# Output weights split in the dense part, two more pairs of tiles turned by DMA, and a new order of the last part

## The chip, the core and the metric

The kernel runs on one core of one Trainium2 chip. The metric is the device time of one execution in microseconds, as the median of the runs. Beside it stands one profiled execution, whose trace gives all the rows below. In the rows PE is TensorE, PEld its weight loads, DVE is VectorE, ACT is ScalarE, POOL is GpSimd and SP is SyncE, which issues most of the transfers.

## The reference

```python
x = A_x                                            # 1 x 2048 x 640
g = sigmoid((x * gate_w).sum(-1, keepdims=True))
q, k, v = heads(x @ wqkv)                          # 32 heads of 20
pq, pk = q @ w_phi, k @ w_phi                      # per head
phi_q = concat(softmax(pq), softmax(-pq))          # 40 per head
phi_k = concat(softmax(pk), softmax(-pk))
kv, z = phi_k^T v, sum(phi_k)                      # per head
o = (phi_q @ kv) / (phi_q @ z + 1e-6)
a = o @ wo
b = silu(x @ w1) @ w2                              # 640 -> 1728 -> 640
return g * a + (1 - g) * b
```

## The kernel before

All matrices are float32. Where full accuracy is wanted an operand is split in two parts: ScalarE casts it to a high part, and GpSimd or VectorE subtracts to get the low part; TensorE then makes three products in place of one.

The program runs in this order: the keys, values and kv of all 16 tiles of 128 rows (order KV); the dense part b (HEAD, O1 to O10, each of them one pair of w1's column tiles beside the products with w2 of the pair before); then TAIL, which ends the dense part and makes the query features of the tiles 12 to 15; and FIN, which makes those of the tiles 0 to 11 and all the output. Rows are handled in eight pairs of tiles (256 rows). PB gives their order: pair 0 of FIN's count is the tiles 12 and 13, pair 1 the tiles 14 and 15, pairs 2 to 7 the tiles 0 to 11.

Each of these parts is an order written out by hand, a string of step names. A step issues its instructions when its name is reached, and a chain of dependencies keeps every engine in that order (in TAIL and FIN also SP's queue, in the dense part not SP). An engine that waits holds back all that stands behind it on that engine, and nothing on the others.

The query features of a tile t: q_proj (TensorE, 30 matmuls, steps qp12 to qp15 and q0p to q11p), q_max and q_sub (VectorE, from PSUM), q_exp (ScalarE), q_sum and q_norm_sum (VectorE), q_norm (GpSimd, the product with z), q_parts, q_inv and q_weights (small ones), q_mul (GpSimd, qm and q0M and so on). The features must then be turned, so that heads lie on partitions. There are two ways. A pair in TPOSE is turned by TensorE: t_mm makes 22 transposes into banks of PSUM, and t_out evicts them on ScalarE. For any other pair q_out (steps qg12, q0g and so on) copies the features on ScalarE as 16-bit halves and writes them to m_d in DRAM, from ScalarE's queue; three transfers q_in (steps such as j0, j12) bring them back turned, from SP's queue.

From the turned features n_mm (steps n00 to n04 for pair 0, four matmuls each) makes the heads' outputs, n_hi and n_lo (h, l) evict them to oT as high and low part, and r_mm, r_hi, r_lo (z0m, z0h, z0l) do the same for a rest of the heads, which r_store writes to r_d and r_place (z0d) brings from there into the gap rows of oT. Both pn and rest tiles are taken from the PSUM tag single, with four banks, as are the output's. When all of a block of oT is there (two pairs, 512 columns, for the blocks 0 to 2; one pair for 3 and 4), w_mm multiplies with wo (steps w00a to w44b), w_add adds b, and w_out stores.

The output weights wo are loaded in TAIL (wo_load, five chunks of 128 rows), split by ScalarE and GpSimd (wo_split), and kept in one large tile, which takes a buffer that the last inputs of the dense part hold until hm013.

Pools used by the change: raw (four tiles for unsplit inputs), w (nine large slots for weights and features), x (seven slots for split inputs).

## Time and profile before

| | us |
|---|---|
| median of 3 runs | 702.77 (702.6 to 703.48) |
| the profiled execution | 704.52 |
| its span, from the first to the last instruction | 702.6 |
| TensorE busy in the span | 694.7 |
| VectorE, GpSimd, ScalarE busy | 464.4, 395.5, 309.4 |
| granted clock of TensorE, mean | 0.998 of full |

The time of the profiled execution is 1.9 us over its span; the median of the runs is 0.2 us over that span. The profile is read in three ways here: the share of each engine, which tells who is busy; the same by stretches, which tells where TensorE has room; and the chain of work that ended last, which tells what released each piece of it. A time in the trace counts from the first instruction of the span.

### The profile page before, as it was taken

The page shows a single profiled execution, that of the slowest core. Times are in us where ns is not written, and L with a number is a line of the kernel's source. Part 1 is how long each engine was busy: PE and PEld are TensorE (multiplying, and loading weights), DVE is VectorE, ACT ScalarE, POOL GpSimd, SP SyncE. Part 2 cuts the span into 40 slices and gives each one's busy share as a digit, 9 for nine tenths or more (in the row PEclk, how much of TensorE's full clock was granted, in tenths as well). Part 3 has the DMA queues.
Part 4 walks back from the last instruction along what each step waited for, and adds up shares of the span by engine and source line. Part 5 has one row for each costly group of instructions (what it writes and reads, how often), then busy time and mean ns, then how long its engine had stood idle before and what let it go on. Part 6 is the DMA issues. An engine that isn't in the chain of part 4 may idle for free.

```text
span 702.6 us, 11974 instructions
## 1 busy us (share of the span) xinstructions
PE 694.7 (99%) x4536; PEld 589.1 (84%) x4536; DVE 464.4 (66%) x769; ACT 309.4 (44%) x552; POOL 395.5 (56%) x303
## 2 busy tenths in 40 slices
...
GB/s 307 144 170 293 310 292 298 280 275 237 184 284 146 199 240 231 73 190 240 298 243 245 139 153 126 78 207 261 35 52 140 111 157 202 211 257 209 218 142 132
DMA packets 88631, 140.70 MB, mean 200 GB/s; under 512 B 38466, under 2 KB 52054, under 8 KB 88574
## 3 DMA queue, kind: packets, MB, share of 16 engines
...
q14 instruction: 21, 0.17, 0.1%
...
## 4 chain that ended last, share of the span: by engine, by line
PE 95%; DMA 2%; DVE 1%; ACT 1%; SPq 0%; issue 0%; DVEq 0%; ACTq 0%
PE kvp L621 18%; PE o L1196 11%; PE o L1237 11%; PE pa L1834 10%; PE a L1107 10%; PE pq L597 9%; PE ph L687 3%; PE b L1107 3%; PE c L1107 3%; PE d L1107 3%; PE o_m L1259 3%; PE pn L1756 2%; PE hp L706 2%; PE kvt L608 2%; DMA oT<-r_d 1%; PE kvp L492 1%
## 5 line engine op out<-in xcount | busy, mean ns | idle before, releaser
L1227 DVE TENSOR_TENSOR acc<-acc,o 128x512 f32<-128x512 f32 x104 | 68.4, 683 | 35.3 <-PE o L1237 35.1
L621 PE MATMUL kvp<-wh,xa 128*128 128x480 f32 (+2 forms) x420 | 90.3, 358 | 0.0
L621 PEld LDWEIGHTS kvp<-wh,xa 128*128 128x128 f32 x420 | 72.8, 188 | 10.0
L1196 PE MATMUL o<-u,w 128*128 128x512 f32 x340 | 80.7, 390 | 0.0
L1834 PE MATMUL pa<-oT,wo 128*128 128x512 f32 (+1 forms) x375 | 73.8, 354 | 2.3 <-DMA oT<-r_d 2.3
L1196 PEld LDWEIGHTS o<-u,w 128*128 128x128 f32 x340 | 63.6, 188 | 13.6 <-DVE acc L1201 0.3
L1834 PEld LDWEIGHTS pa<-oT,wo 128*128 128x128 f32 x375 | 60.5, 191 | 14.0 <-ACT eq L1334 2.3
L1351 POOL TENSOR_TENSOR ez<-eq,zbc 128x1280 f32<-128x1280 f32 x16 | 47.6, 2974 | 22.3 <-ACT eq L1334 17.5
L1123 POOL TENSOR_TENSOR u<-v,u 128x512 fp32r<-128x512 f32 x16 | 20.7, 1296 | 64.0 <-ACT u L1122 64.0
L649 POOL TENSOR_TENSOR ek<-ek,st 128x1280 f32<-128x1280 f32 x16 | 38.3, 2397 | 30.8 <-DVE st L648 18.9
L1121 ACT ACTIVATE v<-v 128x512 f32<-128x512 f32 x33 | 20.9, 632 | 78.2 <-DVE v L1140 36.0
L597 PE MATMUL pq<-wq,xb 128*128 128x320 f32 x360 | 55.1, 310 | 0.0
L597 PEld LDWEIGHTS pq<-wq,xb 128*128 128x128 f32 x360 | 53.3, 188 | 2.0 <-issue 1.5
L1091 POOL TENSOR_TENSOR v<-v,v 128x512 f32<-128x512 f32 x32 | 41.7, 1302 | 13.6 <-DVE u L1123 7.0
L621 PE MATMUL kvp<-wl,xa 128*128 128x480 f32 (+2 forms) x210 | 47.6, 356 | 0.0
L1387 POOL TENSOR_TENSOR eq<-eq,sm 128x1280 f32<-128x1280 f32 x16 | 37.9, 2370 | 15.5 <-DVE sm L1381 15.1
L232 POOL TENSOR_TENSOR xa<-xra,xa 128x512 fp32r<-128x512 f32 (+1 forms) x26 | 28.4, 1114 | 24.1 <-ACT xa L230 17.7
L621 PEld LDWEIGHTS kvp<-wl,xa 128*128 128x128 f32 x210 | 36.6, 188 | 4.8
L1123 DVE TENSOR_TENSOR u<-v,u 128x512 fp32r<-128x512 f32 x25 | 19.9, 798 | 29.6 <-ACT u L1122 28.1
L1107 PE MATMUL a<-xo,wc 128*128 128x512 f32 x132 | 33.5, 389 | 0.0
L1397 ACT COPY ez<-eq 128x2400 uint16<-128x2400 uint16 x10 | 22.0, 2200 | 22.4 <-POOL eq L1387 21.3
L451 ACT COPY v<-kvp 128x340 f32<-128x340 f32 (+1 forms) x30 | 12.4, 423 | 40.8 <-PE kvp L621 22.1
...
## 6 DMA issues: line engine op xcount, KB each, us to landing
...
```

Source lines behind the costliest of these rows:

```text
L597: nc.tensor.matmul(dst, xt[c][:, hx, :], w[:, c, hw, lo : lo + n], start=first, stop=(hx == 1 and c == NC - 1))
L621: nc.tensor.matmul(kv_cols(t, lo, hi), xt[c][:, hx, :], WKV[hw][:, c, w_cols(lo, hi)], start=(n == 0), stop=(n == 3 * NC - 1), skip_group_ ...
L649: return lambda: nc.gpsimd.tensor_tensor(groups(e), groups(e), spread(st[:, 1, :]), op=ALU.mult)
L1091: nc.gpsimd.tensor_tensor(v[i], v[a], v[b], op=ALU.subtract)
L1107: last["mm"] = nc.tensor.matmul(out, lhs, rhs, start=(first and i == 0), stop=(stop and i == len(todo) - 1), skip_group_check=True)
L1123: eng.tensor_tensor(u[:, 1, :], v, u[:, 0, :].bitcast(F32), op=ALU.subtract)
L1196: nc.tensor.matmul(o, lhs, rhs, start=(n == 0), stop=(n == len(todo) - 1))
L1227: nc.vector.tensor_tensor(acc[j][m], acc[j][m], o, op=ALU.add)
L1237: nc.tensor.matmul(o, ws[hw], x()[hx], start=(first and i == 0), stop=(i == len(PASSES) - 1), skip_group_check=True)
L1351: nc.gpsimd.tensor_tensor(ez, Q[t]["e"], zbc, op=ALU.mult)
L1387: nc.gpsimd.tensor_tensor(groups(q["e"]), groups(q["e"]), spread(q["sm"][:, 2 * H : 4 * H]), op=ALU.mult)
L1834: nc.tensor.matmul(pa[:, a, :], wo_tile[0][:, c, hw, ds], o[:, c, ho, :size], start=(i == 0), stop=(i == len(TERMS) - 1),)
```

## The change

- TPOSE loses the pairs 0 and 1: they go through m_d and the transposing transfers. TAIL gets qg12 to qg15 and j0 to j2 (pair 0), FIN gets j10 to j12 (pair 1), and the steps t00 to t15 and f00 to f15 go.
- wo is loaded, split and written to wo_d in DRAM in the phases 6 to 8 of the dense part (steps lo, ho, so, ko; SP, ScalarE, GpSimd, SP); wo_load brings the split chunk, 640 KB, back in TAIL; os0 to os4 go.
- The input loads xl3 and xl4, which were issued ahead of FIN, get places in TAIL.
- TAIL and FIN are ordered anew.

The order O7 and O8 change only by the steps lo1 to lo4, ho1 to ho4, so1 to so4 and ko1 to ko4; they are left out, as is the later part of FIN.

```diff
--- before.py
+++ after.py
@@ -74,12 +74,12 @@
 Y43l v14 Y41h Y42l Y41l e14 xf r14 G43l m14 l14
 """
 TAIL = """
-fl1 xl0 hm012 hp012 fm1 fl2 fm2 ol4 fl5 fl4 fs1 fs2 fm4 fl3 fs4 wa fm0 fm5 fs0 fs5 fm3 W fs3 qp12
-q012 q112 qp13 q013 qe12 os4 qn12 wb hm013 q113 qe13 xl2 qs13 xs2 hm113 hp013 qp14 ol2 q114 q014
-hm112 qs12 qn13 qN13 xl1 os2 xs1 im0 qc13 ia0 qe14 hp113 qn14 qs14 im1 qc12 qP13 qi13 ol1 os1 ol3
-qN12 ol0 km kp qN14 os0 qp15 q015 q115 qw13 hp112 ia1 is0 im2 ia2 qP12 is1 xs0 qi12 is2 qc14 qP14
-qm13 os3 qw12 qm12 qe15 im3 ia3 im4 qn15 ia4 im5 qi14 qw14 qm14 is3 is4 qN15 ia5 ig5 im6 ia6 is5
-qs15 ig6 im7 qc15 ia7 ig7 qP15 qi15 qw15 qm15 im8 ia8 im9 ia9 ig9 is7 ig8 is6
+xl2 hm012 fm0 fs0 wa fl1 xl1 fl5 fm5 fl4 fm4 fs5 hp012 fs4 fm1 fl2 fl3 fm3 xs1 fs3 wb W ol3 fm2 ol0
+fs2 km fs1 hm013 qp13 hp013 im0 qp12 q013 kp q113 qe13 qs13 q012 q112 qc13 hm113 qn13 qN13 qp14 ia0
+hm112 qe12 qn12 hp113 qP13 qs12 qi13 qN12 hp112 qw13 qm13 qc12 q114 im1 qP12 ol1 qi12 ia1 qw12 xl0
+im2 ol4 qm12 q014 qg13 qe14 qp15 qn14 qg12 q015 q115 qe15 qn15 ia2 im3 qs14 qc14 ia3 im4 ia4 qN14
+qP14 qi14 qs15 is0 xl4 ol2 is1 is3 xs2 qN15 is2 is4 im5 qc15 qw14 qm14 ia5 qP15 qi15 qw15 im6 j1 ia6
+j0 qm15 im7 ig5 j2 ia7 im8 ia8 is5 im9 xs0 ig6 ig7 is7 is6 ia9 ig9 qg14 xl3 ig8 qg15
 """
 PASS = """
 h0a wh ka h1a h1b h0b us0 wl uh0 xh1 us1 uh1 ul0 h2a h2b us2 h3a ul1 xh3 uh2 h3b xh0 kb xh4 xl3 xh2
@@ -116,19 +116,19 @@
 c1 P4m o4m P4p o4e P6m o5m P6p w3 o5e P3m P3p o6m o6e P7m P7p o7m o7e o8m o8e Cm o9m o9e Cp
 """
 O6 = """
-t3 P1m 2am s0 2ae w0 P1p P2m t2 w1 1bm 1am 1be h2 P2p h3 t4 y0m l2 P5m 2bm s1 1ae c0 2be l3 P5p P4m
-y1m c1 h4 w2 y0e 6am 6bm w3 P4p P6m 6ae l4 6be 5am y1e P6p 5ae P3m 5bm 7am 5be P3p 7ae 7bm 7be P7m
-4am 4ae 4bm 3am 3bm P7p 3ae 3be Cm 4be Cp
+t3 P1m 2am s0 2ae w0 P1p P2m t2 w1 1bm 1am 1be h2 lo0 P2p h3 t4 y0m l2 P5m 2bm s1 1ae c0 2be l3 P5p
+ho0 P4m so0 ko0 y1m c1 h4 w2 y0e 6am 6bm w3 P4p P6m 6ae l4 6be 5am y1e P6p 5ae P3m 5bm 7am 5be P3p
+7ae 7bm 7be P7m 4am 4ae 4bm 3am 3bm P7p 3ae 3be Cm 4be Cp
 """
...
 NSEV = (3, 5)
-TPOSE = (0, 1, 7)
+WO_AT = {6: (0,), 7: (1, 2), 8: (3, 4)}
+TPOSE = (7,)
 FIN = """
-q0p t11 q0m q0s0 x10l t01 x4s x10s t00 t05 q1p x3s t12 f01 x14l t03 x14s q0s1 q0e q0z q0S f11 t15
-f05 f00 q1m t13 q1s0 f12 x7l f15 z1m z0m n00 f03 z0h q1s1 y03 x5l z1h z1l x6l n01 t02 z0l q0Z t14
-f13 t04 q1e q1z y01 f02 t10 x9l q0P z1s f14 n02 q0i q0k f10 n03 z0s h00 n10 n11 f04 q0M x8l x5s n12
-n14 l00 n13 h10 q1S x7s q2p q1Z n04 h01 h12 q1P h11 q1i q0g q1k q1M x9s l11 h02 l10 l12 l01 l02 z0d
-q1g x8s q2m z1d q2s0 q3p q2s1 q2e q3m q3s0 q3s1 q2S x12l q2z w00a w00b q3e w02a q2Z w02b q2P q2i q2k
-q3S q3z j20 q3Z j21 x6s q3P j22 q4p x13l q3i q3k y02 d02 q2M q2g q5p w01a z2m q4m x11l q3M q4s0 x17l
-n20 o02 q4s1 q5m q3g y00 d00 o00 x11s q4e q4z q5s0 y04 q5s1 n22 w01b z2h z2l n23 z2s n24 n21 w04a
-q5e h20 h22 q4S j30 d01 q4Z q4P q4i q5z j32 q4k l20 h21 l21 w04b q4M q7p q5Z l22 n30 j31 n31 d04
-x13s q5S q4g z3m z3h x15l q5P q5i q5k z3l q7m q5M q7s1 z3s z2d n34 n32 h32 h30 y14 x15s l32 o01 n33
-x12s h31 q6p w03a q5g l30 l31 z3d q7s0 q6m w03b q6s1 q6s0 q7e q7S x16l q6e w14a q7z w10a q6z o04 j41
-q7Z q7P q7i w10b q8p q7k q7M q6S w14b q7g q6Z q6P q6i q6k q6M q9p x17s q8m y11 q8s1 d14 q6g y10 q8s0
-q8e j42 d10 q8z n44 d03 q9m j40 n42 z4m z4h z4l o14 q9s1 n40 n41 h40 n43 h42 h41 o10 w12a w12b o03
-y12 w11a l40 q9s0 q8S w11b x16s q11p j50 j52 j51 q8Z q8P q8i q8k q9e q9z n54 d12 l42 z5m q9Z q9S z4s
-q8M q8g n52 n53 z5h y23 d11 q9P q9i q9k n50 n51 q10p z5l y20 h50 w13a z5s h51 o11 l41 z4d w13b h52
-o12 l50 l51 l52 z5d q11m gl q9M w20a w20b q11s1 y22 y13 q11s0 q10m w23a q9g q10s0 q11e q11z q11S j60
-q10s1 q10e q10S w23b j62 w22a w22b j61 q10z d20 q11Z o20 q11P d23 w24a n60 n61 q11i q11k z6m q10Z
...
+x9l q0p q0m q1p x5l q0s0 z0m q0s1 x4s q0e q1m q0z n00 n01 z0h z0l n02 x3s h00 x5s j12 q1s1 z1m q1s0
+q1e j10 q1z q0Z z0s x7l x6l n03 n10 q0S n04 z1h n11 z1l y01 x8l q0P q0i q0k q1S j11 q1Z q1P q2p l00
+q0M q1i q1k h01 l01 h02 l02 n12 x7s q1M h10 l10 x6s z1s y11 n13 q0g n14 h11 x10l q3p l11 h12 l12 z0d
+q2m x8s q2s0 z1d q1g q2s1 w02a w02b x15l q3m q3s0 q2e q3s1 q2S q3e q2z q3z q2Z q2P w00a q2i q2k x11l
+q3Z q2M q3S x11s w00b q3P q4p j21 q3i q3k q4m y00 d00 j22 x10s q4s1 q5p j20 n20 n21 q2g q3M x14l z2m
+q4s0 x12l y02 d02 o00 o02 x9s q3g q4e q4z q5m q5s0 q5s1 h20 z2h x13l l20 n22 n23 h21 q5e w04a y04
+j30 j32 q4S q5z l21 q4Z q4P q4i q4k q4M w01a w01b j31 x12s w04b q5S d04 z2l q7p d01 q5Z q5P q5i x14s
+x13s q4g q7m w03a o01 z2s z3m z3h z3l z3s n24 n30 q7s0 h22 q5k l22 n31 n32 h30 q7s1 l30 n33 n34 x16l
+h31 l31 z2d h32 q5M q6p o04 q7e q7z l32 w03b q7S z3d w11a w11b q5g q6m w14a x15s q6s1 q6s0 w14b q6e
+y14 q7Z q7P q6S j41 q6z q7i q7k q7M q6Z q6P x17l q8p q9p j40 j42 z4m q6i q6k q7g q8m q8s0 d14 d11
+n40 q6M q6g x16s y03 d03 o03 o14 q8s1 q9m z4h z4l q8e q8S q9s0 q9s1 n41 h40 q8z n44 q9e q9z q8Z q8P
+w10a y10 w12a q8i x17s q8k h42 l42 w10b d10 w12b q8M q11p q9S j50 j52 q9Z z5m y12 n50 n51 q9P q9i
+l40 z5h q8g n42 n43 j51 z4s q9k n54 q9M o10 d12 n52 n53 h51 o11 z5l q11m o12 h50 q10p q11s0 l51 h41
+l41 z5s z4d h52 l50 l52 z5d q9g q11s1 q11e q10m q10s0 q10s1 w13a q10e q11S y22 y23 w13b q11z q11Z
...
@@ -1279,13 +1279,23 @@
 
     wor_raw, wo_tile = {}, []
 
+    wo_d = dp.tile([NC, P, 2, D], F32, name="wo_d")
+
+    def wo_early(c, step):
+        if step == "l":
+            wor_raw[c] = r = raw(f"wo{c}")[:, :D]
+            nc.sync.dma_start(r, wo[c * P : (c + 1) * P, :])
+        elif step == "h":
+            wor_raw[c] = wor_raw[c], wslot(f"woh{c}", F32R).rearrange("p (s d) -> p s d", s=2)
+            nc.scalar.copy(wor_raw[c][1][:, 0], wor_raw[c][0])
+        elif step == "s":
+            r, t = wor_raw[c]
+            nc.gpsimd.tensor_tensor(t[:, 1], r, t[:, 0].bitcast(F32), op=ALU.subtract)
+        else:
+            nc.sync.dma_start(wo_d[c], wor_raw.pop(c)[1].bitcast(F32))
+
     def wo_load(c):
-        wor_raw[c] = r = raw(f"wo{c}")
-        nc.sync.dma_start(r[:, :D], wo[c * P : (c + 1) * P, :])
-
-    def wo_split(c):
-        r = wor_raw.pop(c)
-        split(wo_tile[0][:, c, 0], wo_tile[0][:, c, 1], r[:, :D], "pool")
+        nc.sync.dma_start(wo_tile[0][:, c].bitcast(F32), wo_d[c])
 
     def xq(t):
         if t // 4 == NB - 1:
@@ -1619,6 +1629,9 @@
                     for i in (1, 2, 4):
                         ops[f"p{i}{cc}"] = lambda i=i, cc=cc: x_part(i, cc, XR[cc])
                 new_chunks(0, "x", {4: slot_of(0, 4), 3: lambda: place(10)})
+            for c in WO_AT.get(n, ()):
+                for step in "lhsk":
+                    ops[f"{step}o{c}"] = lambda c=c, step=step: wo_early(c, step)
             if n == NPAIR - 1:
                 for cc in range(2):
                     ops[f"p3{cc}"] = lambda cc=cc: x_part(3, cc, XR[cc])
@@ -1713,9 +1726,9 @@
         ops["W"] = wo_big
         for k in range(NC):
             ops[f"ol{k}"] = lambda k=k: wo_load(k)
-            ops[f"os{k}"] = lambda k=k: wo_split(k)
+        for k in range(5):
+            ops[f"xl{k}"] = lambda k=k: xb_load(k)
         for k in range(3):
-            ops[f"xl{k}"] = lambda k=k: xb_load(k)
             ops[f"xs{k}"] = lambda k=k: xb_split(k)
         for t in range(2 * NP - 4, 2 * NP):
             ops[f"qp{t}"] = lambda t=t: q_open(t, q_proj(t))
@@ -1865,7 +1878,8 @@
     with inorder(PE, DVE, ACT, POOL, SP, prev=chain):
         ops = {}
         for p in range(3, len(XP)):
-            ops[f"x{p}l"] = lambda p=p: xb_load(p)
+            if p > 4:
+                ops[f"x{p}l"] = lambda p=p: xb_load(p)
             ops[f"x{p}s"] = lambda p=p: xb_split(p)
         for u in range(NP):
             if u in TPOSE:
@@ -1903,8 +1917,6 @@
                 if part is q_out and PB.index(t // 2) in TPOSE:
                     continue
                 ops[f"q{b}{name}"] = lambda t=t, part=part: part(t)
-        for p in range(3, 5):
-            ops.pop(f"x{p}l")()
         for name in FIN.split():
             ops.pop(name)()
         assert not ops, list(ops)
```

## Rows read from the trace of the kernel before

**Rows 1.** The page: busy time, share, instructions of TensorE.

```profile
PE 694.7 (99%) x4536; PEld 589.1 (84%) x4536; DVE 464.4 (66%) x769; ACT 309.4 (44%) x552; POOL 395.5 (56%) x303
```

**Rows 2.** Busy us by stretch: PE, PEld, DVE, ACT, POOL, then clock, transfer share, GB/s.

```profile
479.86:541.65 61.79, 61.79 (x353) 54.96 (x351) 44.32 (x81) 30.93 (x57) 37.51 (x34) 1.00 0.31 100
541.65:573.02 31.37, 28.81 (x214) 25.22 (x212) 23.64 (x39) 21.36 (x35) 24.60 (x16) 1.00 0.48 138
573.02:700.00 126.98, 126.12 (x781) 107.34 (x781) 89.68 (x149) 47.08 (x62) 66.69 (x33) 0.99 0.76 198
...
350.00:360.00 10.00, 10.00 (x45) 8.26 (x44) 5.28 (x8) 4.24 (x8) 8.93 (x7) 1.00 0.91 299
420.00:430.00 10.00, 10.00 (x46) 8.28 (x45) 5.29 (x8) 3.59 (x6) 4.11 (x4) 1.00 0.42 124
```

**Rows 3.** The chain that ended last: start us, length us, what.

```profile
541.81 4.39 PE pq L597 x30
...
557.97 3.17 PE pn L1756 x28
...
568.05 4.83 DMA oT<-r_d
...
610.63 4.91 DMA oT<-r_d
...
674.59 2.53 PE pT L1649 x22
```

**Rows 4.** Timeline of TensorE, start us and us; idle before and releaser in brackets.

```profile
573.02 4.35 PE L1834 MATMUL pa<-oT,wo 128*128 128x512 f32 x11 [2.10 <-DMA oT<-r_d]
...
605.95 1.47 PE L1756 MATMUL pn<-fT,kvw 120*64 120x256 f32 x12
...
615.67 0.70 PE L1834 MATMUL pa<-oT,wo 128*128 128x512 f32 x2 [0.21 <-DMA oT<-r_d]
```

**Rows 5.** Stretches behind the wait; columns as in rows 2.

```profile
572.00:574.00 2.00, 0.98 (x4) 0.81 (x5) 2.00 (x4) 0.09 (x1) 1.83 (x1) 0.92 1.01 356
574.00:576.00 2.00, 2.00 (x6) 1.53 (x5) 2.00 (x2) 1.78 (x2) 1.74 (x2) 0.50 0.13 34
576.00:578.00 2.00, 2.00 (x8) 1.64 (x7) 1.83 (x6) 0.00 (x0) 2.00 (x1) 0.72 0.75 171
```

**Rows 6.** Timeline of VectorE, 546 to 567 us.

```profile
546.24 0.82 DVE L581 TENSOR_REDUCE mmq<-pq 128x32 f32<-128x640 f32 x1 [3.70 <-PE pq L597]
...
550.60 1.50 DVE L1338 TENSOR_REDUCE pq<-eq 128x64 f32<-128x1280 f32 x1 [1.34 <-ACT eq L1334]
...
555.11 0.48 DVE L1791 TENSOR_TENSOR rT<-pT,rT 128x128 fp32r<-128x128 f32 x2
...
557.02 0.19 DVE L1365 SCALAR_TENSOR_TENSOR sm<-pq,sm 128x32 f32<-128x32 f32 x1
...
559.11 0.69 DVE L1772 TENSOR_TENSOR oT<-pn,oT 128x512 fp32r<-128x512 f32 x1 [0.69 <-ACT oT L1767]
559.72 1.48 DVE L1338 TENSOR_REDUCE pq<-eq 128x64 f32<-128x1280 f32 x1
561.11 1.48 DVE L1354 TENSOR_REDUCE sm<-ez 128x64 f32<-128x1280 f32 x1
...
563.95 2.21 DVE L1772 TENSOR_TENSOR oT<-pn,oT 128x512 fp32r<-128x512 f32 x4
566.77 0.42 DVE L1772 TENSOR_TENSOR oT<-pn,oT 128x256 fp32r<-128x256 f32 x1 [0.61 <-ACT oT L1767]
```

**Rows 7.** Timeline of GpSimd: the last multiplication of TAIL.

```profile
541.71 2.37 POOL L1387 TENSOR_TENSOR eq<-eq,sm 128x1280 f32<-128x1280 f32 x1
```

**Rows 8.** Timeline of ScalarE: a large copy of q_out.

```profile
566.63 2.20 ACT L1397 COPY ez<-eq 128x2400 uint16<-128x2400 uint16 x1
```

**Rows 9.** Timeline of SP's queue: the transposing transfers of one pair.

```profile
574.93 6.07 SPq L1415 DMA_TRANSPOSE fT<-m_d  x3
```

**Rows 10.** Instructions of tile wo on GpSimd: min, median, max ns, first and last start.

```profile
L232 POOL TENSOR_TENSOR wo<-wo,wo x5: 1574/1584/1590, 501.8 to 526.2; 128x640 fp32r<-128x640 f32 x5
```

23 lines of the change are left out of this document (12 added, 11 removed).

## The prediction

> **What bounds the kernel now.** The first view is the page's table of engines: TensorE is busy for 694.7 of 702.6 us [rows 1]. So the time is TensorE's work plus the few places where it waits. The second view is the table by stretches, because the change works on the end: from 479.86 to 541.65 us (the steps of TAIL) TensorE is never idle; from 541.65 to 573.02 (FIN up to the first output block) it is idle for 31.37 - 28.81 = 2.6 us; after that for 0.9 us, nearly all at the very end [rows 2]. The third view is the chain of work that ended last. It runs through TensorE nearly everywhere; twice it leaves it for VectorE and then for the transfer oT<-r_d, issued at 568.05 and 610.63, which takes 4.83 and 4.91 us to land [rows 3]. The last view is the granted clock: after the wait of 2.10 us that ended at 573.02 [rows 4] it is 0.92, 0.50 and 0.72 in three stretches of 2 us, so it was at 1.2 GHz for a part of them, and (0.08 + 0.50 + 0.28) x 2 = 1.7 us of full clock were lost [rows 5].
>
> **What is removed from TensorE.** A turned pair costs 22 transposes; the one that stands alone takes 2.53 us, 0.115 us each [rows 3]. Two pairs go: 5.1 us. This is the most that TensorE's own work can give: 702.8 - 5.1 = 697.7 us.
>
> The Trainium skill ("TensorE: Matmul & The Clock Gate", section "Part 4: PE-mode transpose") gives about 275 ns for a transpose in one kernel's context. Worked out from that page, 44 of them would be an estimate of 12.1 us; the trace has 277 ns as the duration too, but 0.115 us from start to start, and the step is what leaves the span.
>
> **What takes the place of TensorE in that stretch.** I lay out the new FIN with the durations of the old rows. The projection q0p ends at 546.20, q1p now follows at once and ends at 550.6 (4.4 us each, [rows 3]). Then come z0m, z1m and ten n steps, 12 x 0.45 = 5.4 us (28 matmuls in 3.17 us, four to a step, [rows 3]), and q2p and q3p, 8.8 us. TensorE alone would reach the first output block at 550.6 + 5.4 + 8.8 = 564.8, against 570.9 before (573.02 less the wait).
>
> VectorE's list does not get shorter. Before that block it must do, for two tiles, the max, min and two subtractions (546.24 to 550.60 less the idle of 1.34: 3.0 us a tile), four sums over 1280 (559.72 to 561.11: 1.4 each), two chains of small instructions (557.02 to 559.11 less the idle of 0.69: 1.4 each), two rest evictions (0.48 for both), four oT evictions of 512 (2.21 for four, about 0.6 each with the steps around them) and two of 256 (0.42) [rows 6]: 6.0 + 5.6 + 2.8 + 0.5 + 2.4 + 0.8 = 18.1 us. The old trace agrees: from 546.24 to the end of the last oT eviction at 567.19 are 20.95 us, with 1.34, 0.69 and 0.61 of idle in them [rows 6]. In the new order the second tile's max waits for q1p until 550.6, so 1.4 us are idle and the last eviction would end at 546.2 + 1.4 + 18.1 = 565.7. ScalarE adds a little: q0g, 3.6 us with its issues, stands there ahead of the cast h11 and starts after the multiplication q0M, at about 560.7 (q0k is done at 558.3 by the same sum, then 2.37 on GpSimd [rows 7]); h11 ends at 564.9, and the eviction behind it is 0.3 us late: 566.0. The placing transfer z1d is issued at once: z0d, which in the old trace stood 0.8 us ahead of it, now needs an eviction that ends about 1.4 us earlier. With 4.83 us to landing [rows 3] and 0.3 us around it the first output block starts at 571.1. Before it was 573.02. So the gain there is 1.9 us, not 5.1; the rest turns into TensorE idle, 571.1 - 564.8 = 6.3 us in all where it was 2.6.
>
> Where this idle falls: pn and pr tiles have four banks of tag single. z0m, n00, n02 and z1m or n10 fill them, and n04 needs one that is free only when VectorE has done z1l, which the order puts behind both sums of tile 0. By the sum above that is 550.6 + 1.5 (max) + 0.25 + 1.5 + 2.8 + 0.25 = 556.9. TensorE is there by 553.5, so it waits some 3 us at n04 and the rest at w02a.
>
> **The parts that add work.** (1) q_out for four more tiles: ScalarE, 2.20 us for each large copy [rows 8], some 3.6 with the small copy and the issue of its transfers, 14.4 us in all; twelve evictions of turned tiles and five wo casts go. In TAIL ScalarE is busy for 30.9 of 61.8 us [rows 2], so this hides. (2) m_d landed 8.3 us after the copy began (566.63 to 574.93), and three transposing transfers hold SP's queue for 6.07 us [rows 8, 9]. Pair 0 has it early: its multiplications come before im2, and its banks are wanted 20 us later; nothing. Pair 1 is tight. Its last multiplication ran from 541.71 to 544.08 [rows 7]; five wo subtractions of 1.58 us leave GpSimd's queue ahead of it [rows 10], but its inputs come later, since qp15 stands 2.5 us later; between 536.2 and 544.1, I take 540.7. Then m_d is there at 549.0, the transposes are issued from there, 2.0 us each, and the second (j10, for n10) lands at about 554 to 555. TensorE wants n10 at 553. This costs nothing up to 557, since n04 must wait anyway; with the late end (544.1) it costs 0 to 2 us. (3) On SP, xl3, x9l and x5l stand ahead of j12 and wait for raw tiles that GpSimd's splits free; j12 waits for m_d longer. Behind j12 stand z0s, z1s and the x loads for q2p's successors; these have over 5 us to spare. (4) wo in the dense part: five loads of 320 KB, casts, subtractions, stores and later loads of 640 KB. GpSimd is busy for 8.93 us of 10 at 350, but 4.11 at 420; the transfer share is 0.91 and 0.42 [rows 2]. Per phase it is one or two subtractions of 1.58 us among some 25 us. I take nothing; if the cover fails, one late subtraction delays a sevens operand: 0 to 1.6 us. The raw tiles and the slots of tag w are enough by my count of what lives at once. (5) In TAIL the order puts km right behind the fused weights, and its two banks are free only after fs3's eviction on VectorE: no row shows it; 0 to 1.2 us, I take 0.5. The wo loads now wait on SP until hm013 releases their space, some 8 us earlier than before; nothing queued behind them is wanted before 540.
>
> **After the first block.** TensorE's work to the end is the same: 573.02 to 700. Whether new waits arise is read from the second block. There the old trace has the last pn matmul at 607.42 and the placed rows at 615.54, 8.1 us later; 8.0 us of matmuls stood between, so the wait was 0.21 us [rows 3, 4]. The new order has only q6p and half a block between, 6.0 us. If the placing took 8.1 us again the wait would be 2.1; but the new order puts the three evictions of that pair ahead of q6's max, some 1.5 us earlier. Wait 0.2 to 2.1, I take 0.7, so 0.5 more than before. For the third block the distance is 7.8 us in both; 0 to 1.0, I take 0.
>
> **The sum.** -1.9 (first block) + 0.5 (km) + 0.5 (second block) = -0.9 us of the span. The profiled execution took 704.52 us with a span of 702.6; the runs have a median of 702.77 and I subtract from that: 701.9 us. Between the ends of the terms above it lies from 700.4 to 703.4.
>
> **The rivals.** (B) The first block is not held by VectorE and the placing transfer: TensorE sets the time as it does now, and its 5.1 us come out whole: 697.7. For it: TensorE is at 99%. Against: the 18.1 us of VectorE. It comes about if the placed rows land some 3 us sooner than the two seen; 571.1 then becomes 568, 5 us ahead of 573.02, and the second block's wait goes as well. The two placings that the chain shows, 4.83 and 4.91 us, speak against it [rows 3]. The Trainium skill ("DMA: Bandwidth & Descriptors", section "Anatomy of one DMA — SWDGE (gpsimd) path") gives about 2.0 us of fixed cost for a transfer, which would bring B about. (C) Slower. A block behind the first waits as the first did: 2.1 us at the second block by the placing time of the old trace, and the clock falls, 1.7 us more [rows 5]. With one such wait and the clock lost at the first block as before: 701.9 - 0.5 + 2.1 + 1.7 = 705.2. It decides from the point where the placed rows come about 1 to 2 us after TensorE. For it: less matmul stands between the last pn and that block, and the idle at n04 is long enough for a first fall. Against: VectorE's evictions come sooner. (D) The change does not do what it says: the pair turned by DMA is as late as the pair turned by TensorE, because its multiplication is not earlier (544.1); z1m and n10 wait until about 558, the first block is where it was, and the km wait and the second block eat the rest: 702.8.
>
> **How the numbers follow.** The forecast has 0.42, its own range 700.4 to 703.4. B has 0.23, C 0.22, D 0.13. A difference of 0.2%, 1.4 us, is about what a measurement of this kernel can tell from no change: under 701.4 is faster, over 704.2 is slower. Two fifths of the forecast's chance lie under 701.4. Faster: 0.17 + 0.23 = 0.40. Slower: C and a little of D, 0.24. Same: 0.36. The range leaves one in ten on each side: 697.5 (B) to 705.4 (C).
>
> **What would show it.** Right: 22 transposes in place of 66; an idle TensorE of about 3 us before n04, put down to VectorE; the first output block at 571.1, its wait put down to oT<-r_d; VectorE almost without idle from 550.6 to 566.0. Wrong for B: that block at 568 or earlier. For C: a wait over 1.5 us before a later pa matmul, with the granted clock at 0.5 behind it. For D: a wait at z1m or n10 for fT that lasts beyond 557. A wait in 355 to 430 would show the wo steps at fault, and a start of q0p later than 542.3 the steps of TAIL.

## The result and the profile after

The changed kernel takes 705.68 us (median of 14 runs, 703.43 to 708.35) where the kernel before, in the same comparison, takes 703.19 (701.54 to 704.4): ratio 1.004, 95% interval 1.0024 to 1.0055, so slower by 0.4%. The forecast was 701.9 with a range up to 705.4; the measured time lies just outside it, on the side of rival C. Two executions of the whole study, of 1395 and 2420 us, were in a slow state and are in none of these numbers.

The page of the kernel after, TensorE's line (as in rows 1), shows that the change does what it says: 44 instructions fewer and 5.2 us less of work.

```profile
PE 689.5 (98%) x4492; PEld 584.8 (83%) x4492; DVE 465.0 (66%) x769; ACT 310.8 (44%) x546; POOL 395.6 (56%) x303
```

The profiled execution took 704.71 us with a span of 702.9 us, 0.3 us more than the span of before: all of the 5.2 us came back as idle time. The timeline of TensorE, kernel after, from 300 us on, shows where: these are the groups ahead of which it was idle (start us, us, what; idle before and releaser in brackets), but for one of 0.24 us at 456 that before has too. Before, from 500 us on, these were 0.31, 2.10 and 0.21 us ([rows 4] has the last two), and nothing near 406 or 437.

```profile
406.19 2.32 PE L1237 MATMUL o<-u,w 128*128 128x512 f32 x9 [0.74 <-ACT v L1129]
437.55 0.73 PE L1237 MATMUL o<-ts,sa 128*128 128x512 f32 x2 [0.86 <-POOL ts L1085]
...
485.31 6.23 PE L349 MATMUL pwq<-constb,wTq 40*128 40x40 f32 x50 [0.22 <-DMA wTq<-wqT]
553.87 0.44 PE L1793 MATMUL pr<-fT,kvwr 128*64 128x128 f32 x4 [0.22 <-DMA fT<-m_d]
555.98 0.65 PE L1769 MATMUL pn<-fT,kvw 120*64 120x256 f32 x4 [1.24 <-DMA fT<-m_d]
558.27 1.08 PE L1769 MATMUL pn<-fT,kvw 120*64 120x256 f32 x8 [1.64 <-DVE rT L1804]
559.68 6.17 PE L597 MATMUL pq<-wq,xb 128*128 128x320 f32 x30 [0.32 <-DVE sm L1391]
573.98 7.12 PE L1847 MATMUL pa<-oT,wo 128*128 128x512 f32 x30 [2.09 <-DMA oT<-r_d]
656.20 12.39 PE L1847 MATMUL pa<-oT,wo 128*128 128x512 f32 x53 [1.11 <-DMA oT<-r_d]
```

Read from the top: two waits in the dense part, at steps that the change did not mean to touch; one at the fused weights of TAIL; then z1m, n10 (pair 1's transposing transfers), n04 (the bank that z1l frees) and q2p (the bank that q0k frees); the first output block, later than before (573.98 against 573.02); and a new wait at the third block. q2p takes 6.17 us where a projection takes 4.4 [rows 3]. The stretches of the kernel after (columns as in rows 2) say why: there the clock falls to 1.2 GHz for a part of them, (0.08 + 0.50 + 0.27) x 2 = 1.7 us lost, as much as before lost behind its first block [rows 5]; behind the first block it holds now.

```profile
558.00:560.00 2.00, 1.41 (x9) 0.84 (x10) 1.86 (x8) 1.03 (x3) 2.00 (x2) 0.92 0.84 245
560.00:562.00 2.00, 2.00 (x9) 2.00 (x9) 2.00 (x2) 0.86 (x2) 2.00 (x2) 0.50 0.91 161
562.00:564.00 2.00, 2.00 (x12) 2.00 (x12) 1.86 (x7) 1.93 (x1) 1.28 (x2) 0.73 0.80 180
...
574.00:576.00 2.00, 2.00 (x9) 1.66 (x10) 2.00 (x3) 1.02 (x1) 2.00 (x1) 1.00 0.72 260
```

### The profile page after: what moved, and what is told of

The parts are those of the page before. It is cut to its first block, busy times and chain, and to the rows that moved or that the text cites. A ratio compares the mean times of both kernels' runs of the same rounds, so it can differ in the third digit from the quotient of the medians.

```text
span 702.9 us, 11926 instructions
## 1 busy us (share of the span) xinstructions
PE 689.5 (98%) x4492; PEld 584.8 (83%) x4492; DVE 465.0 (66%) x769; ACT 310.8 (44%) x546; POOL 395.6 (56%) x303
## 4 chain that ended last, share of the span: by engine, by line
PE 85%; DVE 5%; DMA 4%; issue 2%; POOL 2%; ACT 2%; ACTq 0%; SPq 0%; POOLq 0%; DVEq 0%
PE kvp L621 13%; PE o L1196 11%; PE pa L1847 10%; PE o L1237 9%; PE a L1107 8%; PE pq L597 8%; PE ph L687 3%; PE b L1107 3%; PE o_m L1259 3%; PE d L1107 3%; PE c L1107 3%; PE hp L706 2%; PE pn L1769 2%; PE kvp L492 1%; DMA oT<-r_d 1%
## 5 line engine op out<-in xcount | busy, mean ns | idle before, releaser
L1847 PE MATMUL pa<-oT,wo 128*128 128x512 f32 (+1 forms) x375 | 71.8, 349 | 3.3 <-DMA oT<-r_d 3.2
L1123 DVE TENSOR_TENSOR u<-v,u 128x512 fp32r<-128x512 f32 x25 | 21.5, 858 | 30.0 <-ACT u L1122 30.0
L1407 ACT COPY ez<-eq 128x2400 uint16<-128x2400 uint16 x14 | 30.7, 2196 | 21.0 <-POOL eq L1397 21.0
L232 POOL TENSOR_TENSOR xb<-xrb,xb 128x512 fp32r<-128x512 f32 (+1 forms) x18 | 19.8, 1106 | 29.5 <-ACT xb L230 29.5
```

What stands on the lines that cost most here:

```text
L232: eng.tensor_tensor(lo, src, hi.bitcast(F32), op=ALU.subtract)
L1123: eng.tensor_tensor(u[:, 1, :], v, u[:, 0, :].bitcast(F32), op=ALU.subtract)
L1847: nc.tensor.matmul(pa[:, a, :], wo_tile[0][:, c, hw, ds], o[:, c, ho, :size], start=(i == 0), stop=(i == len(TERMS) - 1),)
```

## A second trace of each kernel, and a table by marks

> The changed kernel once more, for a second profile and a tighter time. Theory 1 (the clock): executions of this kernel have the same waits and differ in where the clock of TensorE falls behind them; so the second profile has waits at n10, n04, q2p and the first block within 0.4 us of the first profile's 1.24, 1.64, 0.32 and 2.09, and any difference in span is found in stretches with a granted clock under 1. Theory 2 (the waits themselves vary): the clock is the same and the waits differ by the difference in span. Time 705.7 either way.

> The kernel before once more, for a second trace. Theory S (part of the difference between medians and profiles lies in the first 400 us, where both kernels are the same): the matmuls that stood at 405.79 in the first trace of before come 0.5 to 1.2 us earlier in this one, and the span is shorter by as much, 701.5 to 702.1; the waits behind 400 are those of the first trace, none over 0.4 but the 2.1 at the first block, with the clock falling behind it. Rival: the stretch behind 541 differs from trace to trace, because the clock falls or holds at the first block.

Two profiles whose spans differ by 0.3 us can't explain medians that differ by 2.5, so both kernels were profiled once more. The second trace of before has a span of 700.2 us: it is at the first step of the dense part named below 0.9 us earlier, and the clock holds at its first block, though the wait there is nearly the same (1.98 us). So theory S has its share, and so has its rival. The second trace of after has the waits at n10 and n04 of the first (1.17 and 1.67 us) and loses twice as much clock, 3.4 us, as theory 1 has it; at q2p it shows no wait, and at the block for 1.41 us where theory 1 left room down to 1.7. So the waits vary too. First the timeline of before_again at its first block, then a stretch behind it, then five stretches of again (columns as in rows 2).

```profile
572.06 7.12 PE L1834 MATMUL pa<-oT,wo 128*128 128x512 f32 x30 [1.98 <-DMA oT<-r_d]
```

```profile
574.00:576.00 2.00, 2.00 (x10) 1.67 (x9) 1.97 (x3) 0.94 (x2) 1.76 (x2) 1.00 0.10 23
```

```profile
556.00:558.00 2.00, 0.65 (x4) 0.23 (x4) 2.00 (x2) 1.84 (x3) 2.00 (x3) 0.93 0.36 102
558.00:560.00 2.00, 1.06 (x6) 0.68 (x8) 1.86 (x7) 0.00 (x0) 2.00 (x1) 0.50 0.94 292
560.00:562.00 2.00, 2.00 (x10) 1.24 (x7) 2.00 (x3) 1.89 (x4) 2.00 (x2) 0.50 0.86 155
562.00:564.00 2.00, 2.00 (x10) 2.00 (x9) 1.93 (x5) 1.34 (x2) 1.94 (x2) 0.50 1.05 232
564.00:566.00 2.00, 2.00 (x14) 2.00 (x14) 1.93 (x7) 1.22 (x2) 0.95 (x1) 0.86 0.21 54
```

Each timed execution comes with its mean granted clock, and that shows the same over many. Of 108 executions of before, 49 have 1.000 (median 702.2 us) and 53 have 0.998 (703.5): about half of them lose the clock once. Of 23 of after, none has 1.000; four have 0.998 (704.9), eleven 0.995 (706.0), five 0.993 (707.3). At equal clock, 0.998, after is 1.4 us slower by the four that it has there; I put that down to its waits, and the rest of the 2.5 us to clock that it loses more often. No run parts the two.

The traces are best compared by marks, since the start varies by 1 us from one execution to the next. The marks are the starts of one step of the dense part (the matmuls o<-u,w near 405), of TAIL (ph<-xo,w near 479), of FIN (q0p) and of the first output block (pa), each read from TensorE's timeline. Stretches in us:

| kernel | to dense mark | dense mark to TAIL | TAIL | FIN to first block | first block to end |
|---|---|---|---|---|---|
| before | 405.79 | 73.91 | 61.95 | 31.37 | 129.58 |
| before_again | 404.93 | 73.94 | 61.94 | 31.25 | 128.14 |
| after | 404.62 | 75.75 | 62.65 | 30.96 | 128.92 |
| again | 405.41 | 75.75 | 62.53 | 30.92 | 129.59 |
| wo_only | 405.49 | 75.76 | 62.82 | 32.00 | 129.13 |
| wo_only_fitted | 404.61 | 73.91 | 63.08 | 31.67 | 128.03 |
| dense_moved | 411.74 | 73.92 | 62.72 | 30.79 | 130.63 |
| dense_fitted | 404.77 | 73.87 | 64.07 | 30.31 | 128.98 |
| no_early_split | 405.26 | 73.86 | 67.12 | 31.35 | 128.41 |
| early_j11 | 405.18 | 75.73 | 62.09 | 29.87 | 130.03 |
| early_j11_filled | 405.38 | 75.72 | 62.15 | 29.01 | 128.54 |
| all_four | 405.19 | 73.86 | 62.08 | 30.29 | 130.18 |
| three_mends | 405.19 | 73.88 | 62.10 | 29.33 | 129.00 |

From after and again against the two traces of before: the change costs 1.8 us in the dense part, in every trace the same; 0.6 to 0.7 in TAIL (the ten traces with its order of TAIL unchanged lie between 62.1 and 64.1); it wins 0.3 to 0.4 up to the first block, where 1.9 were forecast; and behind it wins nothing.

## The dense part

> Only the output weights' part of the change: split in the dense part, loaded back in TAIL behind hm013, all else as in the kernel before. Theory L (the late start of FIN comes from the dense part): waits of 0.7 and 0.9 us near 406 and 437 as in the changed kernel, q0p about 0.5 us later than 541.81, time 703.7. Rival (the late start comes from the new order of TAIL): q0p within 0.2 us of 541.81 and 703.2. Third: the five subtractions that leave GpSimd in TAIL let pair 1 come earlier, which takes away part of the 2.6 us of idle in FIN: 702.2.

```diff
-TPOSE = (7,)
+TPOSE = (0, 1, 7)
...
 hp013
+ol4 ol2 ol1 ol3 ol0
```

The first lines are against the changed kernel, the last against the TAIL of before, which this kernel has, as it has FIN of before. Against the kernel before it has wo_early, the loads of split chunks in TAIL and xl3 and xl4 at its end; the rest is the order of before. Measured: 706.48 us, ratio 1.0048 (1.0033 to 1.0064). The part that was costed at nothing is by itself as slow as the whole change. Theory L has its waits: the trace shows both (0.73 and 0.85), and the table puts 1.8 us there. Its price, 703.7, was too low: TAIL and FIN are longer too, by 0.9 and 0.6 us.

What causes the first wait is in the timeline of VectorE at that place, in the kernel before and then in the kernel after, with GpSimd's row of the kernel after behind it:

```profile
405.34 0.69 DVE L1123 TENSOR_TENSOR u<-v,u 128x512 fp32r<-128x512 f32 x1 [1.42 <-ACT u L1122]
405.95 1.88 DVE L1227 TENSOR_TENSOR acc<-acc,o 128x512 f32<-128x512 f32 x3
```

```profile
404.17 1.33 DVE L1123 TENSOR_TENSOR u<-v,u 128x512 fp32r<-128x512 f32 x1 [1.42 <-ACT u L1122]
405.42 1.87 DVE L1227 TENSOR_TENSOR acc<-acc,o 128x512 f32<-128x512 f32 x3
...
403.36 1.57 POOL L1293 TENSOR_TENSOR woh<-wo,woh 128x640 fp32r<-128x640 f32 x1
```

TensorE's next products start 0.1 us after the first of the three evictions ends, 0.68 us into their row, in both kernels (before 406.63 and 406.73, after 406.10 and 406.19), and so in all ten traces that have this wait. So they wait for that eviction. In the kernel after it is late because VectorE's subtraction ahead of it took 1.33 us in place of 0.69: it ran beside GpSimd's subtraction of a chunk of wo (so2) and ended 0.57 us after that one. The copy v on ScalarE, which the profile names as releaser, ended 0.49 us before the products start in the kernel after, and in the kernel before it ended after they had started (406.88); it is not the cause.

The second wait, in the timelines of ScalarE, VectorE and GpSimd of the kernel after, 428 to 438 us:

```profile
428.10 0.72 ACT L1290 CAST woh<-wo 128x640 fp32r<-128x640 f32 x1
431.13 0.60 ACT L1121 ACTIVATE v<-a 128x512 f32<-128x512 f32 x1 [1.12 <-POOL woh L1293]
...
430.04 1.61 DVE L1123 TENSOR_TENSOR u<-v,u 128x512 fp32r<-128x512 f32 x1 [1.79 <-ACT u L1122]
431.57 1.87 DVE L1227 TENSOR_TENSOR acc<-acc,o 128x512 f32<-128x512 f32 x3
433.36 0.68 DVE L1123 TENSOR_TENSOR u<-v,u 128x512 fp32r<-128x512 f32 x1
...
429.52 1.58 POOL L1293 TENSOR_TENSOR woh<-wo,woh 128x640 fp32r<-128x640 f32 x1
434.19 1.30 POOL L1091 TENSOR_TENSOR v<-v,v 128x512 f32<-128x512 f32 x1 [1.07 <-DVE u L1123]
436.22 1.28 POOL L1085 TENSOR_TENSOR ts<-v,ts 128x512 fp32r<-128x512 f32 x1 [0.73 <-ACT ts L1081]
```

From the product at 437.55 the chain goes back over ts and v on GpSimd to u on VectorE at 433.36, and VectorE has no idle there since 430.04. Its subtraction at 430.04 took 1.61 us in place of 0.69; it ended 0.55 us after GpSimd's subtraction of another chunk (so4). It also began some 0.45 us late against TensorE's products, because ScalarE's cast of that chunk (428.10) stands ahead of the silu it needs. The silu at 431.13 had a wait of its own, 1.12 us: it writes a tile of the pool raw, which the chunk loaded at 405 held until GpSimd's subtraction ended at 431.10. But the cast behind that silu was done at 432.38, a microsecond before VectorE came to it. So the raw tile is not on the way to 437.55 in this trace.

> The changed kernel with the steps of the third to fifth chunk of wo at other places of O7 and O8: ho2 so2 ko2 some 7 us earlier, where ScalarE and GpSimd have room; lo3 and lo4 some 5 us later, behind the loads of w; ho4 so4 ko4 some 9 us earlier, so that its raw tile is free before the silu that waits for one. Theory D (the two new waits of 0.74 and 0.86 us in the dense part are the loss): no such wait is left from 400 to 440, all behind them is 1.6 us earlier, time 1.6 us under the changed kernel, 704.1 (ratio 1.0015). Rival F (the loss is in FIN, and what is won ahead of it is lost again at the first output block): the waits go, the block waits 1.6 us longer, 705.7.

```diff
 w3 6be
+ho2 so2 ko2
 l4 l3 P3m
...
 P7m
-ho2
 4am
-so2 ko2
...
 l2 l3
+lo3
 P5m
...
 P6m l4
+ho4 so4 ko4
 6be
```

Measured: 709.39, ratio 1.0099 (1.0084 to 1.0114). The expectation falls, but by its own edit. Both old waits are gone (73.92 from mark to TAIL); the subtraction so2 now stands ahead of l4 and l3 on GpSimd and waits for its cast, 3.92 us, and TensorE waits 4.64 us for ts, 10 us ahead of the dense mark. GpSimd's timeline, then TensorE's:

```profile
397.69 1.53 POOL L1293 TENSOR_TENSOR woh<-wo,woh 128x640 fp32r<-128x640 f32 x1 [3.92 <-ACT woh L1290]
```

```profile
401.71 3.78 PE L1237 MATMUL o<-ts,sa 128*128 128x512 f32 x8 [4.64 <-POOL ts L1085]
```

> The changed kernel with the third to fifth chunk's steps in the dense part at other places: ho2 so2 ko2 behind l3, where GpSimd has 2.8 us free (in dense_moved they stood ahead of l4 and l3 and held these back); lo3 and lo4 behind the loads of w; ho4 so4 ko4 behind l4, so that its raw tile is free before the silu that takes it. Theory D: the waits of 0.74 and 0.86 us go, all behind them comes 1.6 us earlier, time 704.1, ratio 1.0015. Rival F (what is won ahead of FIN is lost again at the first output block): 705.7, ratio 1.004.

As dense_moved, with ho2 so2 ko2 behind l4 l3:

```diff
 w3 6be l4 l3
+ho2 so2 ko2
 P3m
```

Measured: 703.95, ratio 1.0011 (0.9999 to 1.0022), 1.7 us less than the changed kernel by the two medians. Its timeline of TensorE has no wait left between 300 and 480 us but one of 0.23, where before has 0.27. Theory D holds: the dense part's waits are some 1.8 of the 2.5 us. VectorE's two subtractions take 0.69 us again (at 404.32 and 429.11). The steps were moved together, so that it was so2 and so4 rests on the rows above and not on a run of each; the load lo3, moved too, has no part in either chain.

> wo_only with the dense part's steps placed as in dense_fitted. Theory D: the 1.8 us of the dense part go, and of wo_only's loss the 0.8 us in TAIL and FIN stay: 704.2, ratio 1.0015. Rival (the loss in FIN came with the later start and the clock that fell at the first block): 703.2, ratio 1.000. Below 702.5 the part would be a gain by itself.

wo_only with these orders of O7 and O8. Measured: 703.2 where before has 702.34 in the same comparison, ratio 1.0012 (0.9997 to 1.0027). That is the rival's price: of wo_only's 3.4 us over before 2.6 are gone, more than the waits, and ten of its twelve executions keep a clock of 1.000, where wo_only had two of six. The rest is in TAIL (63.08 us), where a wait of 0.84 us for VectorE's eviction of acc appears at 529. Taking five casts and five subtractions out of TAIL wins nothing there by itself.

> The changed kernel without the output weights' part: O6 to O8 as before, wo loaded unsplit in TAIL and split there by ScalarE and GpSimd at places with room in the new order; TPOSE, TAIL's other steps and FIN as in the changed kernel. Theory D: without the dense part's waits the rest of the change is worth 0.5 us less or more: 702.7 to 703.4, ratio 0.999 to 1.0005, with the wait at n10 up to 1.6 us longer because GpSimd has five subtractions of 1.58 us more in TAIL. Rival F (the new FIN is the loss): ratio 1.003 or more.

```diff
-WO_AT = {6: (0,), 7: (1, 2), 8: (3, 4)}
+WO_AT = {}
...
 hm013
+os3
 qp13
```

Four more os steps stand in TAIL, and ol1, ol2 and ol4 have other places there. Measured: 708.58, ratio 1.0087 (1.0069 to 1.0106). Theory D's second half falls: the rest of the change needs the early split. With five casts and subtractions back in TAIL, TensorE waits 2.50 us there at a projection (VectorE's subtraction frees its bank late), and pair 1 comes later. The places of the os steps are this study's own, so it shows that the two parts hang together, not what the best order would give.

```profile
524.92 4.00 PE L598 MATMUL pq<-wq,xf 128*128 128x320 f32 x15 [2.50 <-DVE eq L589]
558.14 0.44 PE L1800 MATMUL pr<-fT,kvwr 128*64 128x128 f32 x4 [1.11 <-DMA fT<-m_d]
...
577.59 7.13 PE L1854 MATMUL pa<-oT,wo 128*128 128x512 f32 x30 [2.36 <-DVE eq L589]
```

## FIN up to the first output block

> The four sums over 1280 elements of the first two query tiles of FIN (tiles 0 and 1) run over 2 of each 20 elements, so VectorE's list ahead of the first output block is some 5 us shorter; the features of these tiles are not the reference's. Theory V (VectorE's list sets the first block): no wait at n04 for VectorE, the last oT eviction near 565, the first block near 570.5 in place of 574.0, time 3.3 us under the changed kernel, 702.4. Theory M (the transfers of m_d and their transposes set it): the wait at n10 stays at 1.2 us and the last pn steps wait for theirs, the block near 573, time 704.7. If the loss lies behind the first block or ahead of FIN: within 0.5 us of the changed kernel.

```diff
-nc.vector.tensor_reduce(sums[t], groups(Q[t]["e"]), ...)
+nc.vector.tensor_reduce(sums[t], groups(Q[t]["e"])[:, :, : 2 if t in (0, 1) else DH], ...)
```

The same for q_norm_sum. Measured: 708.11, ratio 1.0084 (1.0055 to 1.0113). With 5 us less of VectorE's work the block does not come earlier, but 1.1 us later, counted from q0p. The wait at n04 shrinks to 0.49, as expected of theory V, and then the last pn steps wait 2.63 us for pair 1's transposing transfer, as theory M has it. M's price, 704.7, is missed by 3.4 us; the clock falls behind that wait, and what else the time is made of is not shown. TensorE's timeline of short_sums:

```profile
557.23 1.08 PE L1769 MATMUL pn<-fT,kvw 120*64 120x256 f32 x8 [0.49 <-DVE rT L1804]
...
565.90 2.40 PE L1769 MATMUL pn<-fT,kvw 120*64 120x256 f32 x12 [2.63 <-DMA fT<-m_d]
575.22 7.11 PE L1847 MATMUL pa<-oT,wo 128*128 128x512 f32 x30 [1.61 <-DVE mmq L582]
```

VectorE's timeline of the kernel after says the same: its list does not run without idle into the last evictions, it waits for the casts of the last pn steps, which TensorE began at 565.78.

```profile
567.53 1.02 DVE L1785 TENSOR_TENSOR oT<-pn,oT 128x512 fp32r<-128x512 f32 x2 [1.77 <-ACT oT L1780]
```

> The changed kernel with the matmuls of n03 and of n10 issued four times each (the same result written again), 2.7 us of work put where TensorE waits 1.24 us at n10 and 1.64 us at n04. Theory 1 (the idle lets the clock fall at q2p): the granted clock stays at 1.00 from 556 to 566, q2p takes 4.6 us in place of 6.2, n12 starts near 564.3, the first block near 572.5, time 1.5 us under the changed kernel, 704.2. Rival (the fall has another cause, or costs nothing since the block waits for VectorE and the placing anyway): the first block at 574.0, time 705.7 or up to 0.5 over it.

```diff
+AGAIN = {(0, 3): 4, (1, 0): 4}
...
-        for side in range(2):
+        for side in [0, 1] * AGAIN.get((u, i), 1):
```

Measured: 706.91, ratio 1.0068 (1.0046 to 1.0089). The first half of theory 1 holds: with the idle filled the clock stays up and q2p takes 4.64 us. The rival has the second half: the 1.5 us are waited for at the next place, again the transposing transfer, and the clock falls behind the block instead (8.72 us for its 30 matmuls).

```profile
560.25 4.64 PE L598 MATMUL pq<-wq,xb 128*128 128x320 f32 x30 [0.32 <-DVE sm L1392]
566.20 1.51 PE L1770 MATMUL pn<-fT,kvw 120*64 120x256 f32 x12 [1.31 <-DMA fT<-m_d]
574.38 8.72 PE L1848 MATMUL pa<-oT,wo 128*128 128x512 f32 x30 [2.06 <-DMA oT<-r_d]
```

> The changed kernel with j11, the last of pair 1's three transposing transfers, right behind j10 on SP in place of behind two stores and four loads. Theory 2 (in the changed kernel the last pn steps of pair 1 are held by that transfer, which lands near 565.8 and hides behind the slow q2p): issued at about 553.6 it lands near 561; where the clock holds at q2p n12 starts near 564.4 and the first block comes up to 1 us earlier, 704.7; where the clock falls at q2p nothing changes, 705.7. Rival (the transfers are not what holds TensorE): no difference in either case; and the x loads behind it, 2 us later, cost up to 1 us if q4 or q5 waits for them.

```diff
 q1e j10
+j11
 q1z q0Z z0s x7l x6l
...
 q0k q1S
-j11
 q1Z q1P
```

SP's queue of the kernel after shows what this takes away: the three transposes of pair 1 are not issued together; the third stands behind two stores and four loads. Of early_j11 the same:

```profile
549.00 4.60 SPq L1425 DMA_TRANSPOSE fT<-m_d  x2
...
557.62 4.04 SPq L1425 DMA_TRANSPOSE fT<-m_d  x1
```

```profile
548.94 7.23 SPq L1424 DMA_TRANSPOSE fT<-m_d  x3
```

Measured: 704.44, ratio 1.0024 (1.0012 to 1.0037), 1.2 us under the changed kernel. The block comes 29.87 us after q0p in place of 30.96, and that though the clock fell for longer in this trace (0.995 in the mean). So the rival does not fit; nor does theory 2's reason, since n12 did not start earlier. Half a microsecond of the gain stands in TAIL (62.09), which this edit does not touch. What got shorter is the placing transfer: from the end of the last oT eviction to the block 4.0 us, in the traces of after, again, dense_fitted and filled_idle 4.7 to 5.4. But q8g_later, with j11 at its old place, has 4.1 too. Why it varies is not shown.

> early_j11 with the matmuls of n02 issued twice, of n03 four times and of n10 twice (the same results written again): 2.3 us of work where TensorE waits 0.40, 1.68 and 0.55 us. Theory 1 (behind an early j11 the clock's fall at q2p is on the path): the clock stays at 1.00 from 554 to 566, q2p takes 4.6 in place of 6.0, n12 starts near 564.7, the last casts and evictions come 1.3 us earlier, the first block near 571.5, time 1.0 to 1.4 under early_j11, 703.2. Rival (the wait at the block grows by what q2p wins, and the clock falls there in place of at q2p): 704.4 or more.

The edits of early_j11 and filled_idle, with AGAIN = {(0, 2): 2, (0, 3): 4, (1, 0): 2}. Measured: 704.67, ratio 1.0037 (1.002 to 1.0055): no gain over early_j11. The trace confirms 4.64 us for q2p and a block that comes 29.01 us after q0p, 0.9 earlier, with a wait there of 1.68 in place of 0.69. So TensorE is ready for the block 1.9 us earlier, and half of that is waited for there. The rival has the time. Theory 1's price is refuted, its mechanism not: the profiled execution had a clock of 1.000, but four of the nine executions had 0.995 to 0.998, and they took 706.4 to 707.8.

> The changed kernel with pair 1 turned by TensorE again (TPOSE holds 1 and 7): 22 transposes more, 2.5 us of TensorE, right behind q1p, six evictions on ScalarE; no q_out and no transposing transfers for that pair. Theory V (VectorE's list and the placing set the first block): the waits at n10 and n12 for transfers go, that at n04 for VectorE stays or moves, the first block within 0.7 us of 574.0, 705.7. Theory M (pair 1's transfers set it): the first block near 572, 703.9. Rival (TensorE sets it): 2.5 us later, 708.2.

```diff
-TPOSE = (7,)
+TPOSE = (1, 7)
...
 q1p x5l
+t11 t10 t12
 q0s0
+f11
 q0s1
+f10
 x4s
+t13
```

t14 and t15 and their evictions follow in the same way; n03 stands ahead of h00; qg14, qg15 and j10 to j12 go. Measured: 707.56, ratio 1.0064 (1.0049 to 1.0079), nearest to the rival. The transfers' waits go, and z1m, which now comes later, frees its bank later: n04 waits 3.10 us, the block is at 576.09. So turning pair 1 by DMA was the better way in this order.

## The third output block

> The changed kernel with q11m and q11s0, a max of 1.5 us and a subtraction of 0.7 on VectorE, behind the evictions of pair 5 and z5d in place of between them, as it stands for q11m in the kernel before. Theory 3 (the new wait of 1.1 to 1.5 us at the third output block comes from VectorE's list there): that wait falls to 0.3 or less, time 1.0 under the changed kernel, 704.7, ratio 1.0025. Rival (the place is bound elsewhere, and q11's features come 2 us later): the wait moves to q11's pair at the end, 705.7 to 707.

```diff
 z5l
-q11m
 o12 h50 q10p
-q11s0
 l51 h41
...
 z5d
+q11m q11s0
```

Measured: 705.23, ratio 1.0041 (1.0021 to 1.0061). Theory 3 falls: the wait stays at 1.48 us, and VectorE now stands idle for 4.54 us ahead of the eviction. It waits for ScalarE's casts. Timelines of TensorE, VectorE and ScalarE, q11_later:

```profile
656.25 8.04 PE L1846 MATMUL pa<-oT,wo 128*128 128x512 f32 x34 [1.48 <-DMA oT<-r_d]
...
648.97 0.69 DVE L1784 TENSOR_TENSOR oT<-pn,oT 128x512 fp32r<-128x512 f32 x1 [4.54 <-ACT oT L1779]
...
643.91 2.20 ACT L1406 COPY ez<-eq 128x2400 uint16<-128x2400 uint16 x1
646.13 0.54 ACTq L1411 DMA_DIRECT2D m_d<-ez  x1
646.77 1.54 ACTq L1412 DMA_DIRECT2D m_d<-sm  x1
648.35 1.84 ACT L1779 CAST oT<-pn 128x512 fp32r<-128x512 f32 x4 [1.94 <-issue]
```

Between the copy q8g and the casts ScalarE issues the two stores to m_d: 1.94 us in which it does nothing else.

> The changed kernel with q8g, the copy of a tile's features on ScalarE and the issue of its two stores, behind h52 in place of ahead of h51. Theory 4 (the casts of pair 5 wait for ScalarE, behind q8g): the casts start at about 647 in place of 648.3, the placed rows land 1.3 us earlier, the wait at the third block falls from 1.1 to 1.5 us to 0.2 or less, time 1.2 under the changed kernel, 704.5, if pair 6's transposing transfers, 3.5 us later, don't hold n60 (they land some 6 us ahead of it now). Rival (the placing transfer sets it, whatever the casts do): the wait stays over 0.8.

```diff
 l40 z5h
-q8g
 n42 n43
...
 z5d
+q8g
 q9g
```

The wait at the third block is gone from the trace, which settles its cause: theory 4. But the time is 708.19, ratio 1.0062 (1.004 to 1.0084): TensorE is idle for 1.75 us from 668 to 672 and loses 1.7 us of clock behind that. The wait of 1.32 us in it, at n60, is put down to VectorE's eviction of an output tile (669.27; the first of three ends 0.06 us before TensorE goes on). VectorE's list there is late: one of its sums waits 1.55 us for a store to m_d, which it does not in after. Pair 6's transposes come 2.9 us later too, counted from the first block (issued at 662.41, in after at 658.40). The stretches of q8g_later:

```profile
668.00:672.00 4.00, 2.25 (x17) 0.92 (x16) 3.01 (x8) 0.47 (x1) 2.36 (x1) 0.99 0.98 208
672.00:676.00 4.00, 4.00 (x15) 3.35 (x16) 1.09 (x3) 0.87 (x3) 0.00 (x0) 0.58 0.79 255
```

## The mends together

> dense_fitted, early_j11, q11_later and, in TAIL, wa behind fl3 (so that the fused weights' loads don't queue behind its 640 KB). The theory that the change is lost to waits that can be named, each on its own: 1.6 us in the dense part, 0.2 to 0.6 at the fused weights, 1.1 at the transposing transfer, 1.1 at the third block, gives 705.7 - 4.2 = 701.5, ratio 0.9975. Rival (what goes at one place comes back at the next, above all at the first output block): 703.2 or more.

Measured: 701.71, ratio 0.9985 (0.9973 to 0.9996), 4.0 us under the changed kernel and faster than before, by less than the 0.2% that counts as a difference here. The theory of separate waits comes out nearly in full by its sum, 4.0 of 4.2 us, but the third block, 1.1 of it, still waits 2.20 us in its trace: the sum agrees in part by luck.

> all_four without the move of q11m and q11s0: dense_fitted, early_j11 and wa behind fl3. If the three effects add up (1.8, 1.1 and some 0.6 us under the changed kernel) and the move is worth nothing, as when it was made alone: 702.0, ratio 0.9985. If the move matters once the rest is mended: 703.0 or more.

all_four without the move of q11m; the edit of wa in TAIL is

```diff
 xl2 hm012 fm0 fs0
-wa
 fl1 xl1
...
 fl2 fl3
+wa
 fm3
```

Measured: 702.1 against 702.34, ratio 0.9991 (0.9978 to 1.0004). The two intervals overlap; three mends carry it, and q11m's move isn't needed. Without wa's move the fused weights waited 0.15 to 1.54 us for their loads, or not at all, from trace to trace; with it none of four traces has that wait.

In this trace the stretch up to the first block takes 29.33 us (30.29 in all_four), 1.9 to 2.0 less than before: there the 1.9 of the forecast comes out. Behind the block it takes 129.00, 0.9 more than before_again, and none of the twelve executions of three_mends has a clock of 1.000. So even mended the change does not win clear of the noise, with 5.2 us less work for TensorE.

> dense_fitted, early_j11, wa behind fl3 and q8g_later together, without the move of q11m. If the third block's wait of 2.2 us in all_four goes by theory 4 and nothing takes its place: 701.7 - 1.5 = 700.2, ratio 0.996. Rival (the last blocks are held elsewhere): as all_four, 0.9985.

> best with the repeats of early_j11_filled. By theory 1 1.0 to 1.4 under best, 699.0, ratio 0.994; by its rival no difference from best.

three_mends with q8g_later: 702.71, ratio 0.9999 (0.9988 to 1.001); with the repeats too: 703.75, 1.0018 (1.0002 to 1.0033). Both expectations fall, and the rivals come nearer, though both times are still above theirs. What q8g's move wins at the third block it loses at n60 again (a wait of 1.28 us there), and the repeats lose as before.

## Why the forecast was wrong, step by step

- **TensorE's work.** Right: 5.2 us measured for 44 transposes, 0.118 us each, against 0.115 from [rows 3], in two traces that lost about the same clock. The 275 ns of the Trainium skill ("TensorE: Matmul & The Clock Gate", section "Part 4: PE-mode transpose") would have made it 12.1, an estimate from that page; what leaves the busy time is the step, not the duration, which the trace of before has too (277 ns).
- **wo in the dense part, taken at 0 with an upper end of 1.6: the step that failed.** It measured 1.8. The sum priced the subtractions at nothing because GpSimd had room: 4.11 of 10 us at 420 [rows 2]. GpSimd did have it; neither wait is its own. What the step left out is that a subtraction on GpSimd holds up the one that VectorE makes beside it: 1.33 and 1.61 us in place of 0.69, at places where a product of TensorE hangs on VectorE's next step, and once a cast on ScalarE ahead of a silu. "One late subtraction delays a sevens operand" was the right fear with the wrong engine. "The raw tiles are enough by my count" was wrong as well, since a tile that is loaded 23 us ahead of its use is held that long and the next writer waits, but that wait of 1.12 us did not reach TensorE.
- **km and the start of FIN, taken at 0.5.** TAIL took 0.6 to 0.7 longer. Right in size, not in place: with km where it was TAIL takes 62.1, as before, in every trace without a wait at the fused weights; with wa moved there is none.
- **The first block, taken 1.9 earlier.** Measured 0.3 to 0.4. The waits came at n10, n04 and the block, in the order given, and n04's end was right: 558.27 for 556.9 with a start 1.4 later. Wrong is what the stretch ends on. VectorE's list was to run without idle into the last eviction, at 566.0 or, with the late start, 567.4; it ended at 568.55 with 1.77 us of idle ahead of it, and 5 us less on that list move nothing (short_sums). The last pn steps are late instead, and two things hold them, each long enough by itself: the third transposing transfer (next item), and q2p, which took 6.17 us, because the clock fell in idle that rival C named and the sum did not take in. With the fall alone gone they start 22.6 us after q0p (filled_idle), with the transfer alone earlier 23.1 (early_j11), in after 22.8; with both, 21.2. Then half of the gain is waited for at the block.
- **j12, j10, j11 on SP.** "Costs nothing up to 557" looked at n10 alone. The third of the three, which the order puts behind x loads, was not followed to its landing.
- **The second block, taken at 0.5.** The wait was to be 0.2 to 2.1 us. It is too short to show in the first trace of after and 0.32 in the second: at the low end, so the 0.5 did not come.
- **The third block, taken at 0 with an upper end of 1.0.** It waited 1.1 to 1.5 in after and again. The distance in matmuls was counted, and the new neighbour on ScalarE's queue, q8g with its issues, was not.
- **The profile it was read from.** The sum was made against one execution, which had lost 1.7 us of clock at its first block, and left that as it was. About half of before's executions keep it, and the changed kernel loses as much or more in all 23. That difference, some 1.1 of the 2.5 us by the medians at equal clock, is in no term of the sum.
- **The range.** The upper ends that stand beside the terms add 0.7 for km, 1.4 for the second block, 1.6 for wo and 1.0 for the third block to 701.9: 706.6, and not 703.4. The terms allowed the measured time; the range that was made from them did not.
- **Rivals.** B did not come: from the end of the last eviction to the block it took 3.9 to 6.0 us in all twenty traces. The Trainium skill's 2.0 us of fixed cost ("DMA: Bandwidth & Descriptors", section "Anatomy of one DMA — SWDGE (gpsimd) path"), which that section gives for transfers issued by GpSimd, is below all of these; SP issues the ones here. D has the block nearly where it was, but not its sign: n10's wait ended at 555.98, before 557. C has the sign, and of its two causes the clock's fall and a wait at a later block, though the third and not the second. That its 705.2 is near in size is luck, since 1.8 us of the result are in none of the rivals; only the closing list named the place, as "a wait in 355 to 430", and one of the two waits lies in it.
